# Retention with a bilinear feed-forward layer on one core: vector sums moved between VectorE's row stage and its layer

## Chip, cores and metric

One core of a Trainium2 chip. The metric is the device time of one execution in microseconds (us), median of the runs shown. Engines are named as in the profile: PE is TensorE (PEld its weight loads), DVE is VectorE, ACT is ScalarE, POOL is GpSimd, SP is SyncE, which issues most DMAs.

## What is computed

Per head, scores of queries and keys are weighted by a decay to the power of the distance and multiplied by the values (retention, no softmax). The result, 4608 tokens of width 512, goes through a bilinear feed-forward layer of inner width 1536.

```python
scores = scale * np.matmul(q, k.transpose(0, 1, 3, 2))      # B, H, S, D = 8, 8, 576, 64
gamma = 1.0 - 2.0 ** (-5.0 - np.arange(H))
Dmat = np.where(rel >= 0, gamma[:, None, None] ** rel, 0.0) # rel = pos[:, None] - pos[None, :]
attn = np.matmul(scores * Dmat, v)
x = attn.transpose(0, 2, 1, 3).reshape(B * S, H * D)        # 4608 x 512
out = ((x @ w_a) * (x @ w_b)) @ w_out                       # 512 -> 1536 -> 512
```

## The kernel before

The kernel is software-pipelined by hand. PE never leaves the feed-forward layer for long: blocks of tokens (one of 512, two of 256, then seven of 512) pass through it one after another, and in between, at places given by a list `todo` with due times in units of a matmul of 512 columns, PE does *stretches* of retention for the tokens of later blocks.

**A block** of 512 tokens has a layer and a row stage. In the layer (`ffn_block`, L1387 to L1410) there are twelve groups F: four matmuls into a bank `pa` (L1387, x times w_a), a copy by ACT to `ha` (L1398), four matmuls into `pb` (L1405, x times w_b), and a gating product on DVE, `hT = ha * pb` (L1410). `pa` and `pb` come from the pool `ps_ffn`, which has four PSUM banks; a bank is handed out again when its last reader, as recorded so far, is done. So what DVE and ACT have been told to do by then decides which bank comes next, and PE waits for that bank's reader.

**The row stage** (`rows_mixed`) multiplies hT by w_out. From the fifth block on (token 1536) it uses a Winograd-style scheme with seven products instead of eight (84 matmuls `m`, L1045). It needs sums of rows of hT (`row_sums`, L979, on DVE, partly while the layer runs) and sums of w_out made once (`weight_sums`, L960). Order inside: products 3 and 4, copies `straight` by ACT (L1057), product 1; then all DVE work still open (`work(math.inf)`); then `cross` for both halves (products 5 and 2, the copy `crossed` by ACT, L1057, an add to `osb` on POOL, L1068) with `lessen` behind each (DVE, `less`, L1078); then products 7 and 6 and four adds to `osb` on DVE (L1085), which free the banks `m34` for the next block.

**The last two blocks** run four or two of their six double groups by the same kind of scheme (`middle_layer`, `last_layer`, matmuls L1220). They need sums of w_a and w_b, made by `combine` (L1173, tile `combos` or `combo`): sixteen instructions on DVE, each of two bf16 sources in SBUF, for pairs (p, m) with p 0 or 3, m 0 (w_a) or 1 (w_b), and i from 0 to 3, where i = 2 and 3 read earlier results. They also need four sums of x (`combine_rows`, L1190, tile `rows`), made in the row stage ahead of them.

**A stretch** (`stretch(into, outof)`) begins the pair of token tiles `into` and ends the pair `outof`. PE multiplies the state by the queries (L762), keys by values into two banks of `ps_ffn`, kv0 and kv1 (L663), keys by queries (`matched`, L734), and masked scores by values (L775). DVE then makes four running state sums (`add(i)`, L687 and L690, tile `sums`): sums 0 and 2 read kv0, sums 1 and 3 read kv1, and each needs the one before it. Then come two masks (`masked`, L743, tile `sT`) and, on ACT, copies of the states (L693 to L699). Each block of the later part has two stretches: the first with `into` odd, the second, just ahead of the block's last group, with `into` even. Where `into` is one of two special pairs (`LEFT`), there are no state sums.

**The order on DVE** is the order of recording. A stretch records the first `NOW` state sums at once. The rest, the masks, the row sums and the weight sums go as jobs (priority, cost, function) to a list, and `work(budget)`, called behind each hT, records those that fit. State sums have priority 0, weight sums 1.5 to 1.8 and cost 0.5. POOL meanwhile prepares the pairs to come: queries (L578, L583), keys (L604, L608) and values (L615), from f32 tiles that SP's DMAs fill; SP then transposes them (L632).

Of the kernel before, what the change touches and what calls it, by code (L numbers as in the profile page):

```python
# [18 lines left out]
def kernel(  # L19
# [10 lines left out]
    nc = tc.nc  # L30
# [4 lines left out]
    NTOK = B * S  # L35
# [9 lines left out]
    NP = NTOK // 256  # L45
    LEFT = {NP - 3: 0, NP - 1: 1}
    FIRST = 3
    MIXED = 6
# [58 lines left out]
    def ps_next(name, scores):  # L107

        opening.close()
        ps_sc[0] = opening.enter_context(  # L110
            tc.tile_pool(name="sc_" + name, bufs=scores, space=PS))
        ps_o[0] = opening.enter_context(
            tc.tile_pool(name="o_" + name, bufs=1, space=PS))
# [92 lines left out]
    for a in (0, 1):  # L206
        nc.gpsimd.affine_select(
            out=mask_s[64 * a:64 * a + 64], in_=mask_s[64 * a:64 * a + 64],
# [98 lines left out]
    later = []  # L307
# [5 lines left out]
    jobs, copies_due = [], []  # L313
# [8 lines left out]
    def pass_on(count):  # L322
        while copies_due and count:
            copies_due.pop(0)()
            count -= 1
# [399 lines left out]
    def matched(n):  # L725
        qkT = of(transposed, n)
        sc = [ps_sc[0].tile([128, HP, 2, 64], FP32, tag="sc", name=f"sc{on}")
              for on in (0, 1)]
        begun = Begun()
        for c in range(HP):  # L730
            for kp in (0, 1):
                for a, r in QUADS:
                    on = r ^ a
                    nc.tensor.matmul(sc[on][half(a), c, kp, :],  # L734
                                     qkT[half(on), 1, kp, c, half(a)],
                                     qkT[half(on), 0, kp, c, half(a)],
                                     start=begun.first(on, a), stop=True,
                                     skip_group_check=True)
        sT = st_pool.tile([128, 2, HP, 2, 64], BF16, tag="sT", name="sT2")
        scored[FIRST + n, "pair"] = sT  # L740

        def masked(on):
            nc.vector.tensor_tensor(  # L743
                sT[:, on].rearrange("p c k s -> p (c k) s"),
                sc[on].rearrange("p c k s -> p (c k) s"),
                mask3.unsqueeze(1).to_broadcast([128, 2 * HP, 64]),
                op=ALU.mult)
        return masked
# [47 lines left out]
    def open_outputs(n, apart=False):  # L796

        if apart:
            o = [ps_ffn.tile([128, HP, 2, 64], FP32, tag="ab", name=f"os{a}")
                 for a in (0, 1)]  # L800
        else:
            o = ps_o[0].tile([128, 2, HP, 2, 64], FP32, tag="o", name="o2")
        begun = Begun()
        from_states(n, o if apart else [o[:, a] for a in (0, 1)], begun)

        kp = int(0 in (block_of(n, 0), block_of(n, 1)))
        if apart:
            for a in (0, 1):
                nc.scalar.copy(fence[:, a:a + 1], o[a][:, 0, kp, 0:1])
        else:  # L810
            nc.scalar.copy(fence, o[:, :, 0, kp, 0])
        opened[n] = o, begun

    def close_outputs(n):

        o, begun = opened.pop(n)
        apart = isinstance(o, list)
        keys_into(n, o if apart else [o[:, a] for a in (0, 1)], begun)

        def kept(kp):  # L820
            x = rows_at(n, kp)
            if apart:
                for a in (0, 1):
                    nc.scalar.copy(x[:, a], o[a][:, :, kp].rearrange(
                        "p c (s k) -> p c k s", k=2))
                return
            at = o[:, :, :, kp]
            if n < MIXED:
                by = qs_1[:, :, 128 * kp:128 * kp + 128].rearrange(
                    "p c (a s) -> p a c s", a=2)  # L830
                nc.vector.tensor_tensor(x, at, by, op=ALU.mult)
                return
            nc.scalar.copy(x, at.rearrange("p a c (s k) -> p a c k s", k=2))

        later.append(lambda: kept(0))
        later.append(lambda: kept(1))
# [9 lines left out]
    def stretch(into, outof):  # L846

        (settle if into == NP - 1 else flush)()
        if into == FIRST:
            ps_next("pair", 2)  # L850
        if into in LEFT:
            open_outputs(outof, True)
            open_outputs(into)
            masked = matched(into)
            close_outputs(outof)
            later.append(lambda: masked(0))
            later.append(lambda: masked(1))
            return
        if into == 5:
            convert, convert_swapped = keyed(into, False,  # L860
                                             lambda: open_outputs(outof))
            pop()
            pop()
        else:
            if outof is not None and outof not in opened:
                open_outputs(outof)
            convert, convert_swapped = keyed(into, outof is None)
        masked = matched(into)
        if outof is not None:
            close_outputs(outof)  # L870
        if into == 4:
            later.append(later.pop(1))
            behind.extend([lambda: masked(0), convert, lambda: masked(1)])
            behind.extend(convert_swapped(apart=True))
            return
        if into > MIXED:
            for add in later[:NOW]:
                add()
            jobs.extend((0, 0.5, add) for add in later[NOW:4])
            jobs.append((0, 0, lambda: copies_due.extend(  # L880
                [convert, convert_swapped])))
            jobs.extend((0 if into % 2 else 2, 0.7,
                         lambda on=on: masked(on)) for on in (0, 1))
            copies_due.extend(later[4:])
            later.clear()
            return
        later.append(lambda: (convert(), masked(0)))
        later.append(lambda: (convert_swapped(), masked(1)))
# [116 lines left out]
    def rows_mixed(tok0, hT, sums):  # L1005
# [110 lines left out]
        first, rest = range(NP2 - 1), (NP2 - 1,)  # L1116
# [7 lines left out]
                yield from product(g, 1, part, g == 0)  # L1124
        work(math.inf)
        pass_on(math.inf)
        for g in (0, 1):
            yield from cross(g)
            lessen(g)
# [10 lines left out]

    SEVENS = (0, 1, 3, 4)
    COMMON = (0, 1)
    SHARED = 0
    combos = {}

# [3 lines left out]
            "p c (q e f) -> p e c q f", e=2, f=128)  # L1149
        return [[w[:, e, c:c + 2] for c in (0, 2)] for e in (0, 1)]  # L1150

    def combine(p, m, i):

        if (p, m) not in combos:
            shape = [128, 4, 2, 2, 128]
            if p in COMMON:
                if m == 0:
                    both = late["combo"].tile([128, 2] + shape[1:], BF16,
                                              tag="combo", name="combos")
                    combos[p, 0], combos[p, 1] = both[:, 0], both[:, 1]  # L1160
            else:
                combos[p, m] = stage.tile(shape, BF16, tag=("qf", "kf")[m],
                                          name="combo")
            for own in (0, 1):
                if (p, own) in combos:
                    combos[p + 1, own] = combos[p, own]
        (a11, a12), (a21, a22) = quarter_weights(m, p, 2)
        s3, s1, s2, s4 = (combos[p, m][:, k] for k in range(4))
        out, one, other, op = [(s3, a11, a21, ALU.subtract),
                               (s1, a21, a22, ALU.add),  # L1170
                               (s2, a22, s3, ALU.subtract),
                               (s4, a12, s2, ALU.subtract)][i]
        jobs.append((1.5 + i / 10, 0.5, lambda: nc.vector.tensor_tensor(  # L1173
            out, one, other, op=op)))

    row_combos = {}

# [140 lines left out]
    def last_layer(tok0, xT, hT, sums):  # L1318
# [3 lines left out]
        for i, (way, at) in enumerate(ORDER):  # L1322
# [25 lines left out]
            if done is not None:  # L1348
                jobs.extend(row_sums(hT, sums, done, done + 1, SHARED))
            work(SHARE[way])  # L1350
# [149 lines left out]
    rest = []  # L1500
# [45 lines left out]
    starts, at = {}, 0.0  # L1546
# [42 lines left out]
    def third_turn():  # L1589
        for i in (4, 5):  # L1590
            transpose_step(i, (Q, "act"), (K, "dve"))

    todo = [(100, early_casts, ()),
            (112.1, cast_step, (5, Q, "act")),
            (124, third_turn, ()), (128, third_states, ()),
            (136, third_outputs, ())]
# [10 lines left out]
    for n in range(8, NP, 2):  # L1607
# [19 lines left out]
             (411.95, store_held, (2,)), (412.3, load_pair, (11, (K, V))),  # L1627
             (458, load_pair, (12,)), (447, store_held, (2,)),
             (456, store_held, (2,))]
    NOW = 2  # L1630
    LATE = 8, 8, 8, 50, 8
    CAST_A, TURN_A, CAST_B, TURN_B = 96, 58, 96, 58
    for n in range(11, NP):
        casts[n] = placed[n] - (CAST_A if n % 2 else CAST_B)
        turns[n] = placed[n] - (TURN_A if n % 2 else TURN_B)
    for fn, places in ((ahead, casts), (turn, turns)):
        todo += [(at, fn, (n,)) for n, at in places.items()]
    for i in range(16):
        todo.append((starts[NP - 10 + 2 * (i // 4)] + LATE[i // 4]
                     + i % 4 * LATE[4], combine,  # L1640
                     (SEVENS[i // 8 * 2], i // 4 % 2, i % 4)))
    todo.sort(key=lambda e: e[0])

    at = 0.0
# [1 line left out]
    for tb, n in enumerate(blocks):  # L1646
        runs = WCOLS if tb == 0 else [1] * NF
        for cost, edge in ffn_block(tb, tok, n, runs):
            at += cost
            while todo and edge and at >= todo[0][0]:  # L1650
                _, fn, args = todo.pop(0)
# [33 lines left out]
```

## Time and profile before

| | us |
|---|---|
| median of 3 runs (lowest, highest) | 318.87 (318.01, 318.91) |
| the profiled execution | 318.54 |
| its span, first to last instruction | 316.8 |

In this execution the blocks that the change touches lie as follows, read from the rows of PE: row stages at about 145, 179, 212, 244 and 275 us, each some 9 us long; between them the layers, the second last one (`middle_layer`) from 253 to 275 us and the last from 284 to 304 us. The granted clock of PE is 1.0 in all of them.

How to read a row of a timeline: start in us from the begin of the span, length in us, engine, line, operation, written tile `<-` read tiles, shape, how many instructions are merged in the row, and in brackets the idle time of the engine before it and what ended that. A row that merges several instructions shows their joint length. A row by line, without a start, shows the least, median and largest duration in ns of a line's instructions.

### The profile page before, as it was taken

Reading aid. Unit: us, or ns where it says so; the run is one execution under the profiler, and the core shown is the slowest. Engines: PE = TensorE matmul, PEld = TensorE weight load, DVE = VectorE, ACT = ScalarE, POOL = GpSimd, SP = SyncE. Lnnn points to the kernel's source line nnn. Section 1 sums busy time; section 2 is a strip of 40 time slices with the busy share of each in tenths; the row PEclk is TensorE's granted clock in tenths of the full one; section 3 lists DMA queues with packets and bytes.
Section 4 is the critical chain, followed back from the end, with each engine's and each line's share of the span. In section 5 each row is a group of like instructions: output and inputs, shape, how many; then the busy total and the mean of one; then the engine's idle time right before and its main releaser. Section 6 shows DMA issues by size and latency. Waiting matters only on the chain.

```text
span 316.8 us, 9373 instructions
## 1 busy us (share of the span) xinstructions
PE 306.2 (97%) x3836; PEld 191.1 (60%) x3871; DVE 218.7 (69%) x426; ACT 151.0 (48%) x339; POOL 169.6 (54%) x187
## 2 busy tenths in 40 slices
PE   8899999999999999999999999999999999999995
PEld 3554457768544554548654774468545875587774
DVE  5845346767857662579568957886678786859873
ACT  6745346526435454444455535444434555335630
POOL 3990068654994568574796069704990340035313
PEclk9999999999999999999999999999999999999999
DMA  8999999999999999999999986983730030004004
GB/s 213 257 203 207 253 231 194 184 211 179 208 178 222 212 216 204 231 223 280 197 256 218 178 218 139 187 185 77 191 59 11 2 132 2 2 0 134 1 3 132
DMA packets 144795, 50.94 MB, mean 161 GB/s; under 512 B 126576, under 2 KB 141680, under 8 KB 144752
## 3 DMA queue, kind: packets, MB, share of 16 engines
q1 hardware_dynamic: 138272, 45.10, 70.3%
q0 software_dynamic: 5808, 4.72, 9.5%
q8 instruction: 30, 0.49, 0.7%
q10 hardware_dynamic: 672, 0.52, 0.5%
q14 instruction: 13, 0.11, 0.1%
HBM read 37.75 MB, written 9.44 MB: 149 GB/s over the span
## 4 chain that ended last, share of the span: by engine, by line
PE 88%; DVE 3%; issue 2%; DMA 2%; SPq 2%; ACT 2%; DVEq 0%
PE pb L1405 21%; PE pa L1387 20%; PE m L1045 17%; PE po L1431 7%; PE lm L1220 3%; PE pa L1275 2%; PE pb L1275 2%; DMA qf<-in_q_dram 2%; SPq L182 2%; PE ls L1220 2%; PE po L931 2%; PE sc L734 1%; PE o L762 1%; PE o L775 1%; PE kv L663 1%
## 5 line engine op out<-in xcount | busy, mean ns | idle before, releaser
L1410 DVE TENSOR_TENSOR hT<-ha,pb 128x512 bf16<-128x512 bf16 (+1 forms) x96 | 59.3, 618 | 50.0 <-PE pb L1405 43.1
L1405 PE MATMUL pb<-xT,wb_sb 128*128 128x512 bf16 (+1 forms) x382 | 86.9, 352 | 1.0 <-DVE hT L1410 0.7
L1398 ACT CAST ha<-pa 128x512 bf16<-128x512 f32 (+1 forms) x96 | 50.9, 531 | 72.2 <-PE pa L1387 69.5
L1387 PE MATMUL pa<-xT,wa_sb 128*128 128x512 bf16 (+1 forms) x358 | 82.8, 351 | 1.8 <-issue 1.1
L1405 PEld LDWEIGHTS <-wb_sb 128*128 128x128 bf16 x384 | 37.4, 98 | 36.6 <-issue 2.1
L1387 PEld LDWEIGHTS <-wa_sb 128*128 128x128 bf16 x376 | 35.8, 98 | 32.7 <-issue 0.3
L1068 POOL TENSOR_TENSOR osb<-crossed,straight 128x512 f32<-128x512 f32 x12 | 15.2, 1269 | 73.3 <-ACT crossed L1057 53.9
L615 POOL TENSOR_TENSOR vb<-vf,vs 128x1024 bf16<-128x1024 f32 (+1 forms) x17 | 29.4, 1731 | 4.1 <-DMA vf<-in_v_dram 1.9
L578 POOL TENSOR_TENSOR qkb<-qf,qs 64x1024 bf16<-64x1024 f32 x12 | 23.3, 1941 | 15.4 <-DMA qf<-in_q_dram 15.4
L1045 PEld LDWEIGHTS <-hT 128*128 128x128 bf16 x288 | 28.1, 98 | 4.4
L1431 PE MATMUL po<-wo_sb,hT 128*128 128x512 bf16 x113 | 26.7, 379 | 0.8 <-issue 0.6
L583 POOL TENSOR_TENSOR qkb<-qf,qs 64x512 bf16<-64x512 f32 x24 | 25.4, 1077 | 0.7
L1045 PE MATMUL m<-wo_sums,hsum 128*128 128x256 bf16 x216 | 25.7, 273 | 0.0
L1045 PEld LDWEIGHTS <-hsum 128*128 128x128 bf16 x216 | 21.1, 98 | 2.4
L979 DVE TENSOR_TENSOR hsum<-hT 128x512 bf16<-128x512 bf16 (+2 forms) x51 | 22.1, 462 | 0.4
L690 DVE TENSOR_TENSOR sums<-kv,sums 128x256 f32<-128x256 f32 x44 | 18.6, 422 | 2.2 <-DVE sums L687 0.5
L743 DVE TENSOR_TENSOR sT<-sc,mask 128x512 bf16<-128x512 f32 x30 | 19.8, 682 | 0.0
L608 POOL CAST qkb<-kf 64x512 bf16<-64x512 f32 (+1 forms) x34 | 19.2, 592 | 0.9
L604 POOL CAST qkb<-kf 64x1024 bf16<-64x1024 f32 (+1 forms) x17 | 16.1, 945 | 6.1 <-DMA kf<-in_k_dram 5.3
L1431 PEld LDWEIGHTS <-hT 128*128 128x128 bf16 x120 | 11.2, 98 | 12.4
L1078 DVE TENSOR_TENSOR less<-m,crossed 128x512 f32<-128x512 f32 (+1 forms) x14 | 8.3, 613 | 13.2 <-ACT crossed L1057 13.2
L1045 PE MATMUL m<-wo_sums,hT 128*128 128x256 bf16 x144 | 16.9, 273 | 0.0
(159 smaller groups left out, 442.4 us busy)
## 6 DMA issues: line engine op xcount, KB each, us to landing
qf<-in_q_dram SPq DMA_DIRECT2D x32, 256.0 KB, 4.7
vf<-in_v_dram SPq DMA_DIRECT2D x32, 256.0 KB, 5.3
kf<-in_k_dram SPq DMA_DIRECT2D x31, 256.0 KB, 4.9
out_dram<-osb SPq DMA_DIRECT2D x9, 512.0 KB, 3.9
out_dram<-osb SPq DMA_DIRECT2D x22, 128.0 KB, 2.8
wo_sb<-in_moe_w_out_dram POOLq DMA_DIRECT2D x3, 512.0 KB, 16.1
out_dram<-osb SPq DMA_DIRECT2D x6, 256.0 KB, 3.7
qf<-in_q_dram SPq DMA_DIRECT2D x8, 128.0 KB, 3.7
```

Of the source, the lines that this page charges most:

```text
L578: nc.gpsimd.tensor_tensor(per_head(qkb[0:64, Q]), per_head(t[0:64]), by[0:64].unsqueeze(2).to_broadcast([64, 2 * H, D]), op=ALU.mult)
L583: nc.gpsimd.tensor_tensor(per_head(qkb[64:128, Q])[:, 1 - r::2], per_head(t[64:128])[:, r::2], by[64:128, r::2].unsqueeze(2).to_broadcast( ...
L608: nc.gpsimd.tensor_copy(to[:, :, 1 - r], fro[:, :, r])
L615: nc.gpsimd.tensor_tensor(vb[:, e].rearrange("p (h d) -> p h d", d=D), t[:, e].rearrange("p (h d) -> p h d", d=D), decay[:, at], op=ALU.mult)
L743: nc.vector.tensor_tensor(sT[:, on].rearrange("p c k s -> p (c k) s"), sc[on].rearrange("p c k s -> p (c k) s"), mask3.unsqueeze(1).to_bro ...
L979: lambda e=ways[i]: nc.vector.tensor_tensor(*e[:3], op=e[3]))
L1045: nc.tensor.matmul(to, rows, cols, start=(begins and p == 0), stop=True, skip_group_check=True)
L1387: nc.tensor.matmul(pa[:, 0:n], wa_sb[:, c, fs], xT[:, c], start=(c == 0), stop=(c == NC - 1))
L1398: nc.scalar.copy(ha[:, 0:n], pa[:, 0:n])
L1405: nc.tensor.matmul(pb[:, 0:n], wb_sb[:, c, fs], xT[:, c], start=(c == 0), stop=(c == NC - 1))
L1410: nc.vector.tensor_tensor(hT[:, F, 0:n], has[F][:, 0:n], pb[:, 0:n], op=ALU.mult)
L1431: nc.tensor.matmul(po, hT[:, F, u * 128:(u + 1) * 128], wo_sb[:, F], start=(F == 0), stop=(F == NF - 1))
```

## The change

Two things move on DVE. First, of the sixteen weight sums of `combine`, twelve are no longer jobs with due times in the layers. They are recorded directly in the row stages of the five blocks before the last one: three, three, two, two and two, between the masks (the last open work) and the differences (`less`). The other four stay jobs of the second last layer. Second, `NOW` is no longer 2 everywhere: with `into` odd (a block's first stretch) all four state sums are recorded at once, with `into` even (the second) one.

```diff
         if into > MIXED:
-            for add in later[:NOW]:
+            now = NOW[into % 2]
+            for add in later[:now]:
                 add()
-            jobs.extend((0, 0.5, add) for add in later[NOW:4])
+            jobs.extend((0, 0.5, add) for add in later[now:4])
...
         work(math.inf)
         pass_on(math.inf)
+        for sum_ in between.pop(tok0, ()):
+            combine(*sum_, now=True)
         for g in (0, 1):
             yield from cross(g)
             lessen(g)
...
+    EACH = [(p, m, i) for p in SEVENS[::2] for m in (0, 1) for i in range(4)]
+    AT = (3, 3, 2, 2, 2)
+    between, rest = {}, EACH[:]
+    for t, count in zip(range(256 * MIXED, NTOK - 512, 512), AT):
+        between[t], rest = rest[:count], rest[count:]
+    after_these = {t: [rest.pop(0) for _ in range(min(count, len(rest)))]
+                   for t, count in ((NTOK - 1536, 0), (NTOK - 1024, 8))}
...
-        jobs.append((1.5 + i / 10, 0.5, lambda: nc.vector.tensor_tensor(
-            out, one, other, op=op)))
+        def made():
+            nc.vector.tensor_tensor(out, one, other, op=op)
+
+        if now:
+            made()
+        else:
+            jobs.append((1.5 + i / 10, 0.5, made))
...
-    NOW = 2
-    LATE = 8, 8, 8, 50, 8
+    NOW = 1, 4
+    LATE = 8, 50, 8
...
-    for i in range(16):
-        todo.append((starts[NP - 10 + 2 * (i // 4)] + LATE[i // 4]
-                     + i % 4 * LATE[4], combine,
-                     (SEVENS[i // 8 * 2], i // 4 % 2, i % 4)))
+    for t, sums_ in after_these.items():
+        todo += [(starts[t // 256] + LATE[t == NTOK - 1024] + LATE[2] * i,
+                  combine, sum_) for i, sum_ in enumerate(sums_)]
```

More of the change, by code (lines that the diff above doesn't have):

```diff
@@ L1150, in quarter_weights, with combine @@
         return [[w[:, e, c:c + 2] for c in (0, 2)] for e in (0, 1)]
-    def combine(p, m, i):
+    def combine(p, m, i, now=False):
         if (p, m) not in combos:
```

## Prediction

> **What bounds the kernel now.** I read the page first, then the list of waits, then the timelines of PE, DVE, POOL and ACT around each place where PE stands still.
>
> ```profile
> span 316.8 us, 9373 instructions
> PE 306.2 (97%) x3836; PEld 191.1 (60%) x3871; DVE 218.7 (69%) x426; ACT 151.0 (48%) x339; POOL 169.6 (54%) x187
> PE 88%; DVE 3%; issue 2%; DMA 2%; SPq 2%; ACT 2%; DVEq 0%
> ...
> PE pb L1405 <- DVE hT L1410: 0.7, 2, 0.4
> ```
>
> TensorE is busy for 97% of the span and is 88% of the chain that ended last. A change that touches VectorE (DVE) alone can therefore gain only what TensorE now loses to DVE. The waits view names 0.7 us of that: two waits of the second product's bank (pb, L1405) for a gating product of DVE (hT, L1410). The timeline of PE shows more, if starts are subtracted. Four matmuls of a pa or a pb follow the four before them after 0.86 us (161.69 to 162.55 below); anything above that is loss, though the rows overlap and often show no idle time.
>
> ```profile
> 131.52 1.03 PE L1387 MATMUL pa<-xT,wa_sb 128*128 128x512 bf16 x4
> 132.53 1.02 PE L1405 MATMUL pb<-xT,wb_sb 128*128 128x512 bf16 x4
> ...
> 161.69 1.03 PE L1405 MATMUL pb<-xT,wb_sb 128*128 128x512 bf16 x4
> 162.55 1.03 PE L1387 MATMUL pa<-xT,wa_sb 128*128 128x512 bf16 x4
> 163.56 1.02 PE L1405 MATMUL pb<-xT,wb_sb 128*128 128x512 bf16 x4
> ...
> 171.33 1.03 PE L1387 MATMUL pa<-xT,wa_sb 128*128 128x512 bf16 x3
> 172.67 1.02 PE L1405 MATMUL pb<-xT,wb_sb 128*128 128x512 bf16 x4 [0.32 <-DVE hT L1410]
> ...
> 195.88 1.03 PE L1387 MATMUL pa<-xT,wa_sb 128*128 128x512 bf16 x4
> 197.29 1.02 PE L1405 MATMUL pb<-xT,wb_sb 128*128 128x512 bf16 x4 [0.39 <-DVE hT L1410]
> ```
>
> From pa to pb pass 1.01, 1.01, 1.34 and 1.41 us where 0.86 is normal: 0.15, 0.15, 0.48 and 0.55 are lost, 1.33 us in all. These are the only places behind 120 us where a pa or pb starts more than 0.1 us late, apart from the fixed step at the end of each stretch, which the change leaves alone. (The x3 at 171.33 is a row with one record missing.)
>
> Who holds pb there? DVE, with the weight sums of L1173:
>
> ```profile
> 169.30 2.73 DVE L1173 TENSOR_TENSOR combos<-wa_sb,combos 128x512 bf16<-128x512 bf16 x2
> 171.95 0.67 DVE L1410 TENSOR_TENSOR hT<-ha,pb 128x512 bf16<-128x512 bf16 x1
> ...
> 169.79 1.95 POOL L615 TENSOR_TENSOR vb<-vf,vs 128x1024 bf16<-128x1024 f32 x1
> ...
> 193.69 2.09 DVE L1173 TENSOR_TENSOR combos<-wb_sb 128x512 bf16<-128x512 bf16 x1
> 196.56 0.68 DVE L1410 TENSOR_TENSOR hT<-ha,pb 128x512 bf16<-128x512 bf16 x1
> ...
> 193.60 1.90 POOL L615 TENSOR_TENSOR vb<-vf,vs 128x1024 bf16<-128x1024 f32 x1
> ...
> L1173 DVE TENSOR_TENSOR combo<-wa_sb x2: 520/1306/2093, 225.3 to 227.0; 128x512 bf16<-128x512 bf16 x2
> L1173 DVE TENSOR_TENSOR combo<-wb_sb x2: 418/418/419, 274.3 to 274.6; 128x512 bf16<-128x512 bf16 x2
> ```
>
> A weight sum takes 0.42 us alone and up to 2.09 us when a POOL instruction began just before it: the sum at 193.69 ends at 195.78, the POOL product at 195.50. The hT behind it (171.95, 196.56) is late, and pb starts as hT ends (171.95 + 0.67 = 172.62 against 172.67; 196.56 + 0.68 = 197.24 against 197.29).
>
> The two losses of 0.15 us have another cause, a state stretch. Of the four banks that pa and pb share, kv0 and kv1 hold two until the third and the fourth state sum have read them. The second pb behind the stretch must take the bank of the first, and waits for its hT:
>
> ```profile
> L690 DVE TENSOR_TENSOR sums<-kv,sums x44: 407/424/426, 59.1 to 245.4; 128x256 f32<-128x256 f32 x44
> ...
> 159.76 0.69 DVE L1410 TENSOR_TENSOR hT<-ha,pb 128x512 bf16<-128x512 bf16 x1 [0.64 <-PE pb L1405]
> 160.88 0.94 DVE L690 TENSOR_TENSOR sums<-kv,sums 128x256 f32<-128x256 f32 x2
> 162.82 0.69 DVE L1410 TENSOR_TENSOR hT<-ha,pb 128x512 bf16<-128x512 bf16 x1 [1.00 <-PE pb L1405]
> 163.43 0.88 DVE L690 TENSOR_TENSOR sums<-kv,sums 128x256 f32<-128x256 f32 x2
> ```
>
> That hT ends at 163.51, pb starts at 163.56.
>
> **The change part by part.** The built order differs on DVE alone: PE, ACT, POOL and SP run the same instructions in the same order, no DMA moves, and no instruction is added or dropped. What moves is twelve weight sums, and the state sums around one hT in each stretch.
>
> (1) *Twelve weight sums leave the layers of the blocks at 154, 188 and 221 us*, four from each. The hT behind them starts when its pb is done, so the losses of 0.48 and 0.55 us go. The hT has a margin of its own there: each pb needs only the hT two pb earlier, and pb follow each other after 2 x 0.86 us. In the block at 221 us the sums delay no pb now, so nothing is gained there. What is late next is the row sum of L979, which then meets the POOL product that the weight sum met; it can be held for the rest of that product (169.79 + 1.95 = 171.74), under 0.8 us, inside that margin of 1.7 us. Value: -1.03 us, with 0 and -1.03 as ends.
>
> (2) *All four state sums behind a block's first stretch.* At 160 us DVE is free at 159.76 + 0.69 = 160.45. The four sums take 0.94 + 0.88 = 1.82 us, so the third ends near 161.8 and the fourth near 162.3. Banks are now handed out in another order: the second pa behind the stretch takes kv0's bank (needed at 162.55, 0.7 us in hand), the second pb kv1's (needed 0.86 later, 1.1 us in hand), and the hT that held pb is needed one pb later. The 0.15 us go at 132.53 and at 163.56; at 197.29 the same wait is part of the 0.55. The first hT behind the stretch isn't pushed: its pb ends after 162.3 (it started at 162.82). Value: -0.30 us, with 0 and -0.30 as ends.
>
> (3) *One state sum behind the second stretch, three behind the next hT.* Here hT starts no later, and all that stands behind it comes one sum (0.44 us) later. Rows of the row stage:
>
> ```profile
> 149.98 1.28 DVE L743 TENSOR_TENSOR sT<-sc,mask 128x512 bf16<-128x512 f32 x2
> 152.33 1.29 DVE L1078 TENSOR_TENSOR less<-m,crossed 128x512 f32<-128x512 f32 x2 [1.07 <-ACT crossed L1057]
> 154.51 0.76 DVE L1085 TENSOR_TENSOR osb<-m,less 128x256 f32<-128x256 f32 x2 [0.23 <-PE m L1045]
> ...
> 181.81 1.28 DVE L743 TENSOR_TENSOR sT<-sc,mask 128x512 bf16<-128x512 f32 x2
> 184.52 0.69 DVE L1078 TENSOR_TENSOR less<-m,crossed 128x512 f32<-128x512 f32 x1 [1.43 <-ACT crossed L1057]
> 185.83 0.69 DVE L1078 TENSOR_TENSOR less<-m,crossed 128x512 f32<-128x512 f32 x1 [0.62 <-ACT crossed L1057]
> 186.53 0.76 DVE L1085 TENSOR_TENSOR osb<-m,less 128x256 f32<-128x256 f32 x2
> ...
> 189.36 0.81 PE L1387 MATMUL pa<-xT,wa_sb 128*128 128x512 bf16 x3
> ...
> 184.57 2.58 POOL L1068 TENSOR_TENSOR osb<-crossed,straight 128x512 f32<-128x512 f32 x2 [12.83 <-DMA kf<-in_k_dram]
> ...
> 183.91 0.58 ACT L1057 COPY crossed<-m 128x512 f32<-128x512 f32 x1 [0.98 <-PE m L1045]
> ...
> 250.12 0.69 DVE L1078 TENSOR_TENSOR less<-m,crossed 128x512 f32<-128x512 f32 x1 [1.43 <-ACT crossed L1057]
> 253.39 0.88 DVE L1190 TENSOR_TENSOR rows<-xT,rows 128x512 bf16<-128x512 bf16 x2
> 254.56 0.60 PE L1220 MATMUL lm<-rows,combos 128*128 128x256 bf16 x4
> ```
>
> ACT's copies of the states shift with the sums, but ACT stands idle for 0.98 us before its copy at 183.91, which covers 0.44. Value: 0.
>
> (4) *The weight sums stand in the row stage, ahead of less.* DVE idles there for 1.07, 1.43 and 1.43 us before less, and POOL rests for 12.83 us until its add at 184.57, so I price a sum at 0.42 us, the row without a POOL neighbour; the other end is 2.09. First row stage: 149.98 + 1.28 = 151.26, three sums 1.26, less at 152.52 instead of 152.33: 0.19 late, which the idle 0.23 before 154.51 takes up. Second: 181.81 + 1.28 + 0.44 = 183.53, three sums, 184.79 against 184.52: 0.27 late, taken up by the 0.62 idle before 185.83. The third stage has two sums and the gap of the second. Fourth: DVE idles 1.43 us before 250.12; 0.44 + 2 x 0.42 = 1.28 fits. It matters most there, because the first row sum of x is needed by PE at 254.56 and made in the pair that ends at 254.27. The fifth takes two sums beyond those it has now, in an idle time of 2.5 us before its less. If that cover were gone, lateness of less up to 186.53 + 0.76 = 187.29 against the pa at 189.36, 2.07 us, would still cost PE nothing. Value: 0, with +6.3 us as the other end (worked out as the last rival).
>
> Sum: 318.54 - 1.03 - 0.30 = 317.2 us for the profiled execution (its span of 316.8 us and 1.7 us around it, which the change doesn't touch). That execution lies 0.33 us under the median of 318.87 and inside 318.01 to 318.91; I predict **317.2 us**.
>
> **The rivals.** *The wait moves to the banks (A).* The second pa now waits for a state sum. If the four sums begin at 160.88 as now, the third ends near 162.3 and 0.3 us remain; one more hT of 0.69 us ahead of them and pa is 0.4 us late, at each of three first stretches. Against it: without the weight sum, DVE has nothing queued before them. It gives back 0.45 to 1.0 us: 317.6 to 318.2.
>
> *Only what the waits view names (B).* If the two rows of 0.15 us come from something other than hT, or the idle 0.32 and 0.39 are all that DVE costs, 0.7 us go: 317.8. For it: those two rows show no releaser. Against: hT's end and pb's start agree within 0.05 us in all of them.
>
> *It doesn't do what it says (C).* PE starts earlier and stands before the next stretch instead, for the keys or the values from POOL: 318.5. Against: POOL's product at 169.79 is done at 171.74, and the stretch behind it begins at 175.35:
>
> ```profile
> 175.35 0.45 PE L762 MATMUL o<-qkT,states 64*64 64x64 bf16 x32
> ```
>
> So PE may come over 3 us earlier before it has to wait for POOL.
>
> *The sums collide in the row stage (D, slower).* If a sum there takes the 2.09 us that it takes beside POOL, three last 6.3 us against 1.07 us of idle time: less comes 5.2 us late, 2.07 us are covered, and PE stands 3.1 us in each of the two stages with three sums: 318.54 - 1.33 + 6.3 = 323.5. It beats the gain from 1.27 us per sum on. Against it is POOL's rest of 12.83 us. The decisive start is that of the third sum: near 184.4, with POOL's add at 184.57, so the margin is 0.2 us; missed, one sum is held for one add (2.58 / 2 = 1.29 us), which the 2.07 us still cover. The Trainium skill ("SBUF — State Buffer", section "SBUF: two separate sides") says that VectorE and GpSimd share a pair of ports under an exclusive lock, which whoever starts first keeps for its whole instruction, and counts a VectorE instruction with two inputs in SBUF among those that need it. By that rule a sum that is late for POOL's add waits all of it, as in D; the trace agrees in the layers (2.09 us beside 1.90), and its row for the row stage is still to come.
>
> **How the numbers follow.** Forecast 0.62 (317.2, 316.8 to 317.6), A 0.14, B 0.10, C 0.06, D 0.08. The three runs before spread by 0.9 us, so about 0.3% (0.96 us) can be told from no change. Faster by more: the forecast and half of A, 0.69. Within: half of A, B and C, 0.23. Slower: 0.08. The range from 316.6 to 318.4 holds the forecast with the scatter of runs, A and B; above it lie C and D.
>
> **What would show it.** In the changed profile pa to pb should be 0.86 us at all four places, and the wait of pb for hT gone from the list; the moved sums should each take about 0.42 us between the masks and less, with POOL idle; less at most 0.3 us behind ACT's crossed copy. It is wrong if pa or its weight load waits for the state sums (A), if pb is still late with hT on time (B), if PE waits for keys, values or states (C), or if sums of 1 to 2 us stand in the row stages (D).

## The result, and the profile after

The changed kernel takes 316.95 us (median of 15 runs, 316.77 to 318.12); the kernel before took 318.56 us (15 runs, 317.72 to 320.13). The ratio is 0.9952 [0.9939, 0.9964], a gain of about 1.5 us. On a second occasion, beside the experiments below, it was 0.9968 [0.9956, 0.998] (317.11 against 318.12 us), a gain of 1.0 us. The profiled execution took 317.11 us, where 318.54 us stood before.

From the page of the changed kernel, the busy time of the engines and the shares of the chain that ended last:

```profile
PE 305.5 (97%) x3836; PEld 191.2 (61%) x3871; DVE 213.1 (68%) x426; ACT 150.9 (48%) x339; POOL 169.4 (54%) x187
PE 92%; DMA 2%; issue 1%; POOL 1%; SPq 1%; DVE 1%; ACT 0%; DVEq 0%; POOLq 0%
```

DVE runs the same 426 instructions in 213.1 instead of 218.7 us: the sums wait less for POOL. In the chain, DVE falls from 3% to 1% and PE rises from 88% to 92%.

PE's list of waits in the changed kernel, complete (engine, tile and line, releaser: us in all, times, longest us). Line numbers behind the edit have moved: L1387, L1405, L1410, L1173 are now L1402, L1420, L1425, L1184.

```profile
PE w L1471 <- DVE idxp_f L227: 1.5, 1, 1.5
PE pa L1402 <- issue: 1.1, 7, 0.2
PE po L1446 <- issue: 0.6, 4, 0.2
PE sc L407 <- ACT qkT L393: 0.5, 1, 0.5
PE tp L389 <- ACT own L450: 0.4, 1, 0.4
```

The wait of pb for hT is gone and nothing has come in its place: no wait for a state sum, a key, a value or osb. (PE's weight loads wait once for a state sum, 0.2 us near 79 us, as they do in the kernel before.) The timeline of PE at the four places:

```profile
131.56 1.03 PE L1402 MATMUL pa<-xT,wa_sb 128*128 128x512 bf16 x4
132.42 1.03 PE L1420 MATMUL pb<-xT,wb_sb 128*128 128x512 bf16 x4
...
162.44 1.03 PE L1402 MATMUL pa<-xT,wa_sb 128*128 128x512 bf16 x4
163.30 1.03 PE L1420 MATMUL pb<-xT,wb_sb 128*128 128x512 bf16 x4
...
171.07 1.03 PE L1402 MATMUL pa<-xT,wa_sb 128*128 128x512 bf16 x3
171.94 1.03 PE L1420 MATMUL pb<-xT,wb_sb 128*128 128x512 bf16 x4
...
195.11 1.03 PE L1402 MATMUL pa<-xT,wa_sb 128*128 128x512 bf16 x4
195.98 1.03 PE L1420 MATMUL pb<-xT,wb_sb 128*128 128x512 bf16 x4
```

From pa to pb pass 0.86, 0.86, 0.87 and 0.87 us. Set beside the prediction's rows of the same matmuls, the starts keep a running account: +0.04 us at the first pa (131.56 for 131.52), -0.11 at the second (162.44 for 162.55), -0.26 at the third (171.07 for 171.33), -0.77 at the fourth (195.11 for 195.88), -1.31 at its pb (195.98 for 197.29), -1.4 at the end of the span (315.4 for 316.8). The steps are 0.15, 0.15, 0.5 and 0.55: the four losses. The 0.09 us that are left appear at one place, behind the next stretch (a pa at 208.85 for 210.26).

DVE in the changed kernel, behind a first stretch and where the weight-sum pair of 2.73 us stood:

```profile
160.25 1.86 DVE L690 TENSOR_TENSOR sums<-kv,sums 128x256 f32<-128x256 f32 x4
...
170.34 1.45 DVE L980 TENSOR_TENSOR hsum<-hT 128x1024 bf16<-128x1024 bf16 x1
```

The four state sums are one block of 1.86 us that begins at 160.25, not at 160.88, as nothing stands before it. The row sum at 170.34 is now the one held by POOL (1.45 us; POOL's product runs from 169.33 to 171.24), as foreseen, and the pb at 171.94 is still on time. The row stages, on DVE and POOL:

```profile
150.98 0.75 DVE L1184 TENSOR_TENSOR combos<-wa_sb 128x512 bf16<-128x512 bf16 x2
151.65 0.42 DVE L1184 TENSOR_TENSOR combos<-wa_sb,combos 128x512 bf16<-128x512 bf16 x1
152.13 1.29 DVE L1079 TENSOR_TENSOR less<-m,crossed 128x512 f32<-128x512 f32 x2
...
152.18 2.50 POOL L1069 TENSOR_TENSOR osb<-crossed,straight 128x512 f32<-128x512 f32 x2 [6.32 <-ACT crossed L1058]
...
183.03 0.76 DVE L1184 TENSOR_TENSOR combos<-wb_sb 128x512 bf16<-128x512 bf16 x2
183.80 2.58 POOL L1069 TENSOR_TENSOR osb<-crossed,straight 128x512 f32<-128x512 f32 x2 [12.57 <-ACT crossed L1058]
```

The third sum of the first stage starts 0.53 us ahead of POOL's add (151.65 to 152.18). In the second stage the last sum starts near 183.37 (the joint row ends at 183.79 and a sum takes 0.42), 0.43 us ahead. All take 0.42 us, those of the other stages too. How near that is to an edge, and what lies behind it, is what most of the experiments ask.

### The profile page after: what moved, and what is told of

Its sections match the earlier page's. It is cut to its first block, busy times and chain, and to the rows that moved or that the text cites. A ratio compares the mean times of both kernels' runs of the same rounds, so it can differ in the third digit from the quotient of the medians.

```text
span 315.4 us, 9369 instructions
## 1 busy us (share of the span) xinstructions
PE 305.5 (97%) x3836; PEld 191.2 (61%) x3871; DVE 213.1 (68%) x426; ACT 150.9 (48%) x339; POOL 169.4 (54%) x187
## 4 chain that ended last, share of the span: by engine, by line
PE 92%; DMA 2%; issue 1%; POOL 1%; SPq 1%; DVE 1%; ACT 0%; DVEq 0%; POOLq 0%
PE pb L1420 23%; PE pa L1402 22%; PE m L1046 17%; PE po L1446 8%; PE lm L1235 3%; PE pa L1290 2%; PE pb L1290 2%; DMA vf<-in_v_dram 2%; PE ls L1235 2%; PE po L932 2%; PE sc L734 2%; PE o L762 1%; PE kv L663 1%; PE o L775 1%; SPq L182 1%
## 5 line engine op out<-in xcount | busy, mean ns | idle before, releaser
L1425 DVE TENSOR_TENSOR hT<-ha,pb 128x512 bf16<-128x512 bf16 (+1 forms) x96 | 59.4, 620 | 59.6 <-PE pb L1420 50.8
L1420 PE MATMUL pb<-xT,wb_sb 128*128 128x512 bf16 (+1 forms) x382 | 86.9, 352 | 0.3
L1402 PE MATMUL pa<-xT,wa_sb 128*128 128x512 bf16 (+1 forms) x358 | 82.7, 351 | 1.7 <-issue 1.1
L1420 PEld LDWEIGHTS <-wb_sb 128*128 128x128 bf16 x384 | 37.5, 98 | 35.2 <-issue 0.3
L1402 PEld LDWEIGHTS <-wa_sb 128*128 128x128 bf16 x376 | 35.8, 98 | 32.4 <-DVE sums L690 0.2
L1046 PE MATMUL m<-wo_sb,hT 128*128 128x256 bf16 x144 | 16.9, 273 | 0.0
```

Of the source, the lines that this page charges most:

```text
L1046: nc.tensor.matmul(to, rows, cols, start=(begins and p == 0), stop=True, skip_group_check=True)
L1402: nc.tensor.matmul(pa[:, 0:n], wa_sb[:, c, fs], xT[:, c], start=(c == 0), stop=(c == NC - 1))
L1420: nc.tensor.matmul(pb[:, 0:n], wb_sb[:, c, fs], xT[:, c], start=(c == 0), stop=(c == NC - 1))
L1425: nc.vector.tensor_tensor(hT[:, F, 0:n], has[F][:, 0:n], pb[:, 0:n], op=ALU.mult)
```

## The experiments

My theory was that of the prediction's sum: weight sums that meet POOL delay hT (0.48 and 0.55 us), the state sums' hold on two banks costs 0.15 us three times, and the new place is free as long as the sums come before POOL's add. The rivals were that one half of the change does all of it, that DVE simply has less to do in the layers, and that the new place has a price which only luck hides.

**Each half alone.** First the weight sums moved, the state sums as before.

```diff
-    NOW = 1, 4
+    NOW = 2, 2
```

> The weight sums in the row stage as in the changed kernel, NOW = 2 for both stretches as before. Own theory (two separate causes): the losses behind the weight sums go (0.48 us, and 0.40 of the 0.55), but the wait of the second pb for the first one's hT, 0.15 us, stays behind each of three first stretches (near 130, 162 and 195 us): about 0.45 us over the changed kernel, 317.4 (ratio to before near 0.997). Rival 1 (the state sums make most of the gain): near 318.2. Rival 2 (A: the new order of the banks gives nothing or costs): not slower than the changed kernel, 316.95 or less.

317.61 us, ratio 0.9986 [0.9975, 0.9997] against 318.11 before. PE's timeline at the place where 0.55 was lost:

```profile
195.49 1.03 PE L1402 MATMUL pa<-xT,wa_sb 128*128 128x512 bf16 x4
196.50 1.02 PE L1420 MATMUL pb<-xT,wb_sb 128*128 128x512 bf16 x4
```

1.01 us from pa to pb: 0.15 us stay there, as they do at the two other first stretches, with every weight sum out of these layers. So the bank's share is real, and it is three times 0.15, the third inside the 0.55. The ratio falls short of the 0.997 that was expected: the median gains 0.5 us, not the 0.88 that is -1.03 less the 0.15. "Is the 0.48 us always there?" below bears on that. Then the state sums alone, in the kernel before:

```diff
-            for add in later[:NOW]:
+            for add in later[:NOW[into % 2]]:
...
-    NOW = 2
+    NOW = 1, 4
```

> NOW = 1, 4 as in the changed kernel, the weight sums in the layers as before. Own theory: the parts don't add up. The 0.15 us go near 132 and 163 us, the 0.48 stay, and near 196 us the second pa now waits for the third state sum, which stands behind a weight sum of 2.09 us: it ends near 197.1, so pa is some 1.2 us late where pb was 0.55 late. Sum: -0.30 + 0.65 = +0.35, near 318.9 (ratio 1.001), with a wait of PE for the state sums in the list. Rival (the parts add): -0.3 to -0.45, near 318.2 (ratio 0.9988), no such wait.

318.85 us, ratio 1.0027 [1.0014, 1.0039]: this half alone is slower. DVE and PE at the third first stretch:

```profile
193.28 2.10 DVE L1173 TENSOR_TENSOR combos<-wb_sb 128x512 bf16<-128x512 bf16 x1
195.30 1.85 DVE L690 TENSOR_TENSOR sums<-kv,sums 128x256 f32<-128x256 f32 x4
...
194.60 1.03 PE L1405 MATMUL pb<-xT,wb_sb 128*128 128x512 bf16 x4
196.75 1.04 PE L1387 MATMUL pa<-xT,wa_sb 128*128 128x512 bf16 x4 [1.12 <-DVE sums L690]
```

pa is due at 195.46 and starts at 196.75, 1.29 us late, when the third of the four sums is done. This is rival A, the wait that moves to the banks, and the condition is the one the prediction gave: something must stand ahead of the state sums, here a weight sum of 2.10 us. (At the stretch near 160 us a weight sum that is not held, 0.42 us, stands ahead of them, and PE loses nothing.) The expectation that the 0.48 us would stay failed: the pair of weight sums was recorded one hT earlier and delayed no pb. The parts do not add: -0.14% and +0.27% alone, -0.32% together on the second occasion.

**Is it their load on DVE, or POOL?** The kernel before, with the twelve weight sums that the change moves replaced, at their old places, by an instruction that reads nothing. The kernel so leaves out these sums, and its last two layers work with constants in their place.

```diff
-            out, one, other, op=op)))
+            out, one, other, op=op) if (p, m) == (3, 1) else
+            nc.vector.memset(out, 0.5)))
```

> The kernel before with the twelve weight sums of the layers replaced by memsets of the same tiles in the same places (about 0.49 us each by the row of ones); so the last two layers work with constant weights in place of those sums. Own theory: it is not DVE's load but the meeting with POOL's instructions that makes a sum last up to 2.09 us; a memset reads nothing and lasts 0.4 to 0.5 us everywhere, hT is on time, and as in the first kernel of this call only the three waits of 0.15 us stay: near 317.5 to 317.7. Rival 1 (load: any instruction of DVE there makes hT late): near before, 318.3 to 318.6. Rival 2 (a memset is held by POOL as well): durations to 2 us and near 318.6.

317.55 us, ratio 0.9989 [0.9977, 1.0001], the time of the kernel with the sums moved. The same place as above, DVE and POOL:

```profile
193.38 0.48 DVE L1175 MEMSET combos<- 128x512 bf16 x1
193.07 1.90 POOL L615 TENSOR_TENSOR vb<-vf,vs 128x1024 bf16<-128x1024 f32 x1
```

It runs in the middle of POOL's product and takes 0.48 us where a sum took 2.09. All twelve take 0.48 us, and no pb waits for them: twelve instructions at the old places do no harm if POOL does not hold them. It was the meeting with POOL that cost, not the load. The three losses of 0.15 us stay here too (pb comes 1.01 us behind pa at 132.43, 163.46 and 196.44), so the length of the weight sums is not what causes them.

**Is the 0.48 us always there?** The kernel before once more, one profile.

> The kernel before, for a second profile. Own theory: the meeting of a weight sum with a POOL instruction hangs on tenths of a microsecond, so the two waits of pb of 0.48 and 0.55 us can come out larger or smaller by some tenths, while the waits of 0.15 us, which hang on the order of the instructions alone, come back at the same two places unchanged. Rival (all four are fixed by the order): the same four losses to 0.05 us.

Its DVE, POOL and PE at the third and the fourth place:

```profile
169.12 1.25 DVE L1173 TENSOR_TENSOR combos<-wa_sb,combos 128x512 bf16<-128x512 bf16 x2
170.18 1.95 POOL L615 TENSOR_TENSOR vb<-vf,vs 128x1024 bf16<-128x1024 f32 x1
...
171.15 1.03 PE L1387 MATMUL pa<-xT,wa_sb 128*128 128x512 bf16 x3
172.02 1.03 PE L1405 MATMUL pb<-xT,wb_sb 128*128 128x512 bf16 x4
...
195.24 1.03 PE L1387 MATMUL pa<-xT,wa_sb 128*128 128x512 bf16 x4
196.66 1.02 PE L1405 MATMUL pb<-xT,wb_sb 128*128 128x512 bf16 x4 [0.39 <-DVE hT L1410]
```

317.84 us. The 0.55 us is as it was, and so are the two losses of 0.15 us (pb at 132.36 and 163.39, 1.01 us behind pa); the pair near 169 takes 1.25 instead of 2.73 us and pb comes 0.87 us behind pa. Here POOL's product began at 170.18, when the second sum had started; in the prediction's rows it began at 169.79, ahead of it. So one of the four losses is a matter of tenths of a microsecond between two engines. It may be why one comparison gave 1.5 us and the other 1.0, and why the weight sums alone gained 0.5 us and not 0.88; that is not shown, as only two executions of the kernel before have a profile.

**Four state sums everywhere.**

```diff
-    NOW = 1, 4
+    NOW = 4, 4
```

> The changed kernel with NOW = 4, 4: all four state sums behind the second stretch too, so that hT comes behind them. Own theory: the place of the state sums in the second stretch matters to nothing; hT ends near 179.2 to 179.6 while the row stage needs that group at 180.0: within 0.1 us of the changed kernel, 316.9 to 317.1. Rival (one sum there is part of the gain): at least 0.1 us per second stretch, 317.3 or more, with a wait of PE for hT at the begin of the row stages.

318.91 us, ratio 1.0032 [1.0021, 1.0043]: the whole gain and more is gone, and the expectation with it. PE's waits, and PE and DVE around the second stretch of the block at 154 us:

```profile
PE m L1046 <- DVE sums L690: 1.1, 3, 0.6
...
177.76 1.03 PE L1420 MATMUL pb<-xT,wb_sb 128*128 128x512 bf16 x4
179.08 2.79 PE L1046 MATMUL m<-wo_sums,hT 128*128 128x256 bf16 x24 [0.29 <-DVE sums L690]
```

The first product of the row stage is due at 177.76 + 0.86 = 178.62 and starts at 179.08. With all four sums recorded, kv's bank counts as the next to come free and goes to the row stage, which must then wait for the sum that reads it. It happens in three row stages and costs 0.46, 0.36 and 0.76 us there, 1.6 of the 1.8 us by which the median lies above the changed kernel's 317.11. The step from two sums to one behind the second stretch, on the other hand, does nothing:

```diff
-    NOW = 1, 4
+    NOW = 2, 4
```

> The changed kernel with NOW = 2, 4: two state sums behind the second stretch, as before the change, four behind the first. Own theory: the banks of the row stage go by what is recorded by then; with two sums recorded neither kv bank is free yet, as with one, so nothing changes: the changed kernel's ratio (0.9968 in the last call) within 0.001, and no wait of PE at the row stages. Rival (the step from two to one is part of the gain): 0.1 us or more per second stretch, ratio 0.998 or above.

317.07 us, ratio 0.9964 [0.995, 0.9978], as the changed kernel, and PE waits for no state sum.

**The price of the row stage.** Each moved sum is made twice, the second time over the first.

```diff
-            made()
+            for _ in range(2):
+                made()
```

> The changed kernel with each of the twelve weight sums in the row stages made twice (same result). Own theory: in a stage with three sums the fourth to sixth start just as POOL's two adds do; one or two of them are held by an add of 1.29 us, less comes 1.0 to 2.5 us late, of which about 2 us are covered: PE loses 0 to 0.5 us in all, 316.9 to 317.4, and the trace has sums of over 1 us in the row stages. Rival 1 (no collision in the row stage): sums of 0.42 us, less 1.0 us late, no loss. Rival 2 (less has no cover): 1 us per three-sum stage and more, 319 or above.

324.93 us, ratio 1.0219 [1.0197, 1.0242], where at most 0.5 us was expected. DVE, POOL and PE in the first row stage:

```profile
151.24 2.74 DVE L1184 TENSOR_TENSOR combos<-wa_sb 128x512 bf16<-128x512 bf16 x4
153.90 3.53 DVE L1184 TENSOR_TENSOR combos<-wa_sb,combos 128x512 bf16<-128x512 bf16 x2
157.35 1.28 DVE L1079 TENSOR_TENSOR less<-m,crossed 128x512 f32<-128x512 f32 x2
...
152.43 2.67 POOL L1069 TENSOR_TENSOR osb<-crossed,straight 128x512 f32<-128x512 f32 x2 [6.31 <-DMA vf<-in_v_dram]
155.06 2.08 POOL L578 TENSOR_TENSOR qkb<-qf,qs 64x1024 bf16<-64x1024 f32 x1
...
154.87 1.03 PE L1421 MATMUL pb<-xT,wb_sb 128*128 128x512 bf16 x4
159.34 1.14 PE L1403 MATMUL pa<-xT,wa_sb 128*128 128x512 bf16 x4 [3.45 <-DVE osb L1086]
161.99 1.79 PE L1403 MATMUL pa<-xT,wa_sb 128*128 128x512 bf16 x4
```

Three sums take 0.42 us each; the fourth falls behind POOL's add of 152.43 and takes 2.74 - 3 x 0.42 = 1.5 us; the last two take 3.53 us together. POOL has three instructions here and DVE has three sums against them: each sum waits for the POOL instruction that began before it, and then the next POOL instruction has begun. less comes at 157.35, and PE, due at 155.73, starts at 159.34: 3.6 us lost. A second place costs 2.1 us (PE at 195.98). These two make 5.7 of the 7.9 us by which the span is longer than that of the changed kernel beside it (323.1 against 315.2). Most of the rest lies right behind the first place: from the group at 159.34 on, the next three start at 160.28, 161.99 and 163.61, after 0.94, 1.71 and 1.62 us where 0.86 is normal, 1.7 us more, and the granted clock of PE in this stretch is 0.50 (160.5 to 163.0 us), where it is 1.0 before and after. No other run here has such a fall inside the kernel, and no other has so long an idle time of PE behind 120 us (3.45 us; the next longest, over all runs, are 2.33 and 1.95). That the long wait causes the fall is suggested by this one case, not shown.

**The same instructions behind less**, where POOL's adds have begun.

```diff
-        for sum_ in between.pop(tok0, ()):
-            combine(*sum_, now=True)
         for g in (0, 1):
             yield from cross(g)
             lessen(g)
+        for sum_ in between.pop(tok0, ()):
+            combine(*sum_, now=True)
```

> The changed kernel with the twelve weight sums recorded behind the two less of a row stage instead of ahead of them. Own theory: there POOL is at its two adds, so a sum there is held (1 us and more), the adds to osb come 1 to 2 us late, which their margin of 2.07 and 1.6 us mostly covers; in the fourth and fifth row stage the sums of x come behind them with a margin of only 0.7 us, and PE loses 0.3 to 1 us in each: 317.5 to 318.7. Rival (any place in the row stage is as good): 316.95 within 0.1.

323.5 us, ratio 1.0164 [1.0135, 1.0192]: the direction as expected, the size not. PE's wait, and the rows of DVE and PE in the first row stage:

```profile
PE pa L1402 <- DVE osb L1086: 4.8, 3, 2.3
...
155.33 2.12 DVE L1184 TENSOR_TENSOR combos<-wa_sb,combos 128x512 bf16<-128x512 bf16 x1
157.37 1.40 DVE L1086 TENSOR_TENSOR osb<-m,less 128x256 f32<-128x256 f32 x4
...
154.81 1.03 PE L1420 MATMUL pb<-xT,wb_sb 128*128 128x512 bf16 x4
158.16 1.02 PE L1402 MATMUL pa<-xT,wa_sb 128*128 128x512 bf16 x4 [2.33 <-DVE osb L1086]
```

The second pa starts 158.16 - 155.67 = 2.5 us late, because its bank is freed by osb, which stands behind the held sums. The loss falls in the first three stages (2.5, 2.0 and 0.8 us), not in the fourth and fifth, where I had looked for it. The same twelve sums, recorded behind one loop instead of ahead of it, cost 6.4 us.

**How near the edge is.** Two other divisions of the twelve sums.

```diff
-    AT = (3, 3, 2, 2, 2)
+    AT = (4, 4, 0, 2, 2)
```

> The changed kernel with the weight sums shared out as 4, 4, 0, 2, 2 over the five row stages instead of 3, 3, 2, 2, 2. Own theory: the fourth sum starts 0.05 to 0.2 us before POOL's add or just misses it; in the second case it lasts 1.3 to 1.5 us and less is 1.5 us late, inside the cover of 1.6 us that the doubled sums showed. Either way the ratio stays within 0.001 of the changed kernel's. Rival (any sum beyond three costs PE): 0.3 us or more in each of the first two stages, ratio 0.9985 or above.

```diff
-    AT = (3, 3, 2, 2, 2)
+    AT = (5, 3, 0, 2, 2)
```

> The changed kernel with 5, 3, 0, 2, 2 weight sums. Own theory: in the first row stage the fifth sum is held by POOL's first add (1.3 to 1.5 us) and less comes 1.4 to 1.7 us late, at the edge of the cover of 1.6 us: 0 to 0.2 us lost. If the fourth just misses the add as well, the fifth is held by POOL's second add, less is 3.0 us late and PE loses about 1.4 us before the second pa of the next layer, ratio near 1.001. Rival (only DVE's load counts, 0.42 us per sum): no loss, the changed kernel's ratio.

Four and four: 317.19 us, ratio 0.997 [0.9957, 0.9983]. DVE and POOL in its second stage:

```profile
183.61 1.90 DVE L1184 TENSOR_TENSOR combos<-wb_sb,combos 128x512 bf16<-128x512 bf16 x2
183.96 2.68 POOL L1069 TENSOR_TENSOR osb<-crossed,straight 128x512 f32<-128x512 f32 x2 [12.12 <-DMA kf<-in_k_dram]
```

The fourth sum misses POOL's add by 0.1 us and is held for it (1.90 for two sums), and PE loses nothing behind it. In the first stage the fourth sum starts 0.1 us ahead of the add (152.52 and 152.60) and is not held. Five and three: 318.13 us (317.03 to 318.94, a wide scatter), ratio 0.999 [0.9974, 1.0005], nearly all of the gain gone. DVE, POOL and PE in its first stage:

```profile
153.41 1.49 DVE L1184 TENSOR_TENSOR combos<-wb_sb 128x512 bf16<-128x512 bf16 x1
154.82 1.28 DVE L1079 TENSOR_TENSOR less<-m,crossed 128x512 f32<-128x512 f32 x2
...
153.14 2.89 POOL L1069 TENSOR_TENSOR osb<-crossed,straight 128x512 f32<-128x512 f32 x2 [6.31 <-ACT crossed L1058]
...
155.58 1.03 PE L1420 MATMUL pb<-xT,wb_sb 128*128 128x512 bf16 x4
156.82 1.02 PE L1402 MATMUL pa<-xT,wa_sb 128*128 128x512 bf16 x4 [0.21 <-DVE osb L1086]
```

The fifth sum is held for 1.49 us and PE's pa is 156.82 - 156.44 = 0.38 us late (156.44 is 155.58 + 0.86). This is all that the trace puts down to the fifth sum. PE was 0.5 us behind the changed kernel's profile before it (pb at 155.58 for 155.06), and 0.7 us already at 17 us, where nothing differs between the two programs; so how much of the 1.0 us in the median is the sum's is not shown. No version was measurably faster than the changed kernel.

## Why the prediction was right

The predicted sum, 1.33 us out of the profiled execution, came out as 1.4 us between the two profiled executions. The four losses went by their own sizes, and nothing new stood in their place.

- **Step 1, twelve weight sums leave the layers (-1.03 us).** Right, and the cause is shown: the kernel with the sums moved and the kernel with memsets at the old places take the same time, 317.6 us. But 0.15 of its 0.55 stays unless the state sums move too, as step 2 says, and the term was read from one execution, and its 0.48 us is not there in every one (0 in the second profile of the kernel before). That the first profile held it is chance. Read from the second, the sum would have been 0.85 us and the forecast 317.84 - 0.85 = 317.0 us: the forecast of the time does not hang on it, the size of the gain does. The step might have seen that: in its own rows the product that held the pair began at 169.79, in the midst of the pair, so that 0.4 us later it would have held neither sum.
- **Step 2, four state sums behind the first stretch (-0.30 us).** Right, with its condition. 0.15 us per first stretch stays whenever the state sums stay, and rival A, at 1.29 us in one place, is what comes of the edit if a held weight sum stands in front. The halves of this change need each other.
- **Step 3, one sum behind the second stretch (0).** Right: two or one makes no difference. But that is not because the place does not matter, as my expectation for four sums had it: with four sums there, the banks go round in another order and PE waits for them in three row stages.
- **Step 4, sums in the row stage (0).** The value was right, its reserve was overstated in two ways. The cover of 2.07 us was worked out in the second stage and used for all. In the first stage less and POOL's add both wait for ACT's crossed copy, and in the changed kernel less starts 0.05 us ahead of the add (152.13 and 152.18). In the five-and-three kernel it was therefore due at 153.09 and came at 154.82, 1.73 us late, of which PE lost 0.38: the cover is 1.35 us. With the sums doubled it was due at 152.38, came 4.97 us late, and PE lost 3.61: 1.36 us. (In the second stage, of some 5.0 us, 193.99 for POOL's add at 189.07, PE lost 2.1: there the cover is more than 2.07.) And "one sum is held for one add" is right for the first sum that misses (1.49 us); but every sum behind it is held as well, by the next POOL instruction.
- **The rivals.** A, B and C are out: PE waits for no state sum, the two losses of 0.15 us went with the order of the state sums, and no later wait took up the gain. D did not happen, but its mechanism is real: with six sums in a stage PE lost 3.6 and 2.1 us, where D's price was 3.1 us for each. The rule that the prediction took from the Trainium skill ("SBUF — State Buffer", section "SBUF: two separate sides") agrees with the rows read here: sums with two inputs in SBUF are held to the end of the POOL add or product that began first, 1.4 to 2.1 us, and a memset, which reads nothing, is not (0.48 us).

What stays open: the frequency of the 0.48 us, what else made the five-and-three runs slow, why the granted clock fell in the doubled kernel, and the cause of the last 0.09 us of the 1.4.

## What to carry to other kernels

Subtract the starts of an engine's like instructions from one another before you believe its list of waits: the list named 0.7 us here, the subtraction 1.33, and 1.4 were gained between the two profiles. Read a second profile of the same kernel before you call a loss fixed: one of the four was absent there. Before an instruction moves to a place where the other engine rests, work out the margin to the end of that rest for the last of the moved ones, and count the loss for all that miss it, not for one. Two edits that touch the same buffers are tried apart and together; here one half loses and the whole wins.

## What was not expected of the hardware

DVE and POOL, each with several instructions queued that read SBUF, took turns one for one: sums of 0.42 us came to 1.5, 1.5 and 2.0 us each beside adds and a product of POOL, and 0.1 us between two starts (POOL's add at 183.96, a sum just behind it) decided about a microsecond. Whether the scatter of the runs follows from that is not shown. It is 2.4 us between the lowest and highest time of the kernel before and 1.9 us with five sums in a stage, which stands on that edge, against 1.35 us for the changed kernel, of which 14 of 15 runs lie within 0.45 us. But a part of it arises elsewhere: in the profiles of the five-and-three kernel and of four state sums everywhere, the first layer of the kernel begins at 17.37 and 17.52 us, in the changed kernel's at 16.70, and up to there the programs are the same.
